# Fewer bit steps for the converted weights, and a new split of small steps over two engines, in a fused attention and two-layer expert kernel

## The chip, the core and the metric

The kernel runs on one core of a Trainium2 chip. The core has a matrix engine (TensorE, PE in the rows; its weight loads are PEld), a vector engine (VectorE, DVE), a scalar engine (ScalarE, ACT) and GpSimd (POOL). SyncE (SP) issues most of the DMA transfers. The metric is the device time of one execution in microseconds (us); lower is better. Each engine works through its own list of instructions in the order in which the program recorded them, so an instruction that has to wait holds up all that stand behind it on its engine.

## The reference, cut to what matters

```python
# q, k, v: (2, 8, 768, 64); x: 1536 tokens of 512 numbers
k_sum, v_sum = k in blocks of 32 .max, v in blocks of 32 .mean
scores = [scale * q k^T within a window of 16 | scale * q k_sum^T + log 32]
a = softmax(scores);  x = a @ [v | v_sum]
h = max(max(x @ w1, x @ w2), x @ w3);  x = h @ w_out        # these weights come as float64
score = x @ w_skip;  e = argmax(x @ w_gate)                 # 8 experts
out = x + gate * relu(x @ moe2_w1[e]) @ moe2_w2[e]   where score > 0, else x
```

The routing decides by sign and by largest value, so products are formed from split operands: each operand is a high part plus a low part, and a product is the three matmuls high·high, high·low and low·high.

## The kernel before, in words

**Stages.** The work comes in four groups of 384 tokens (u = 0 to 3). Per group there are four attention units (u, p) with two heads each. A unit is: scores on TensorE (`scores`), masking and row maximum on VectorE (`ttr`), exponentials on ScalarE (`ex`), sums inverted on VectorE (`rec`), normalisation (`norm`, L260), transposes on TensorE (`turn`, L265) with their evacuation (`turned`, L270), the product with the values (`pv`, L278; `fill_v`, L214, fills its summary rows), and the high and low part of the result (`put_h` L286, `put_l` L289). Then come 18 "chains" of 12 matmuls per group (L337: a weight tile (j, f), j = 0 to 2, f = 0 to 5, against the group's x), whose maximum over j gives h; `h_high` (L351) and `h_low` (L354) split h; and `x2_mm` (L364) multiplies by w_out. `route` sorts the tokens to experts and `scatter` (L536) writes their numbers to a table in device memory with indirect DMAs.

**Weight tiles.** 24 tiles of 128x512 float64 numbers (18 for w1 to w3, 6 for w_out) are turned into a float32 high part `wh` and low part `wl` on the chip, from the two 32-bit halves of each number. Per tile ScalarE makes the absolute value of the upper half (`w_c1`, L309) and the rounded top bits of the lower half (`w_r`, L305); a clamp follows on GpSimd (`w_cb`, L313); VectorE then shifts and masks (L317), puts the sign and exponent bit back (L318) and adds the lower bits as integers (L322); the high part is a copy (`w_c4`, L326) on ScalarE or GpSimd and the low part a subtraction on VectorE (`w_c5`, L330).

**What sets the order.** Every step is an entry of the list OPS with an engine. The table HOME names the engine for entries that can run on two (else ScalarE), and the table ORDER lists all entries in the order in which they are recorded. Both tables are constants. 20 entries are warm-up matmuls (`warm_up`, 63 matmuls of 512 columns in all, L159), which compute nothing that is used.

**Opening, middle, seam, last part.** Until 65 us the attention of groups 0 and 1 and the first weight tiles run side by side; the chains of group 0 begin there. After that the chains fill TensorE. At about 285 us the ordered part ends (the seam): the experts' chosen weight chunks (16, in `raw0` to `raw15`) have been split into `wh` and `wl` by `split` (L736, L738), in the buffers that the chains have freed, and the first `pair` starts. A pair puts 256 tokens through one expert: `first` (L1093) is 12 matmuls for each of eight column blocks, `second` (L1105) six each. It begins with the high and low part of the transposed tokens (`put_x`, xth on ScalarE, L712; xtl on VectorE, L713) and, at block 5, transposes the tokens of the next pair (`turn_x`, L705), which GpSimd has fetched by indirect DMA (`fetch`, L718). In GpSimd's list the three scatters of group 3 stand before that fetch. Its waits are for the transfer before.

Of the kernel before, what the change touches and what calls it, by code (L numbers as in the profile page):

```python
# [7 lines left out]
F32 = mybir.dt.float32  # L8
# [110 lines left out]
def build(tc, a, out):  # L119
# [138 lines left out]
    def norm(u, p, h):  # L258
        pr = ST["pr", u, p, h][0]
        nc.gpsimd.tensor_tensor(pr, pr, ST["se", u, p][:, h].unsqueeze(2).broadcast_to([P, TPG, KT]), ALU.mult)  # L260
# [50 lines left out]
    def w_cb(j, f):  # L311
        x = ST["cx", j, f]
        nc.gpsimd.tensor_scalar(x, x, HIGH, LOW, ALU.min, ALU.max)  # L313

# [1096 lines left out]
```

## Time and profile before

| what | us |
|---|---|
| three runs | 446.93, 448.0, 448.46 (median 448.0) |
| the profiled execution | 448.98 |
| its span, first to last instruction | 447.2 |
| PE busy in the span | 432.3 (97%) |
| DVE, ACT, POOL busy | 233.1, 184.3, 138.1 |
| share of PE in the chain that ended last | 83% |

The chain that ended last goes back from the last instruction to whatever released each step. Busy times of matmuls are modelled, so a PE that is called busy may still hold small waits. A "busy" duration of a DVE or ACT instruction overlaps the next one's by some 0.1 us.

### The profile page before, as it was taken

The numbers are of one execution on the slowest core, as the hardware profiler recorded it, in microseconds if no ns is written. First come the engines' busy times: TensorE is split into PE (matmuls) and PEld (weight loads), VectorE is DVE, ScalarE is ACT, GpSimd is POOL, SyncE is SP. The second block draws the span as 40 slices with busy tenths as digits, with TensorE's granted clock in tenths as the row PEclk, the third lists the DMA queues.
The fourth block names the chain that finished last, engine by engine and source line by source line (L and its number), as shares of the span: only waits on it lengthen the run. The fifth ranks groups of instructions, "written<-read, shape, count | busy, mean of one in ns | idle before, by whom it ended". The sixth has DMA issues, their size and how long they took to land.

```text
span 447.2 us, 9609 instructions
## 1 busy us (share of the span) xinstructions
PE 432.3 (97%) x3558; PEld 389.2 (87%) x3558; DVE 233.1 (52%) x738; ACT 184.3 (41%) x507; POOL 138.1 (31%) x191
## 2 busy tenths in 40 slices
PE   8999999999999999999999999799999999999995
PEld 3668889999789999998999999798989889798874
DVE  4899998989852531043214235868226651232321
ACT  3798984743685754107121037211114521212210
POOL 0666561434222522011601322131316034140400
PEclk9999999999999999999999999989999999999999
DMA  8987556456434512003042390242852193010111
GB/s 281 270 304 247 185 169 221 162 178 200 153 131 128 161 42 75 2 0 122 2 113 77 94 331 1 78 65 49 269 203 94 49 301 128 25 52 2 47 49 32
DMA packets 27584, 56.91 MB, mean 127 GB/s; under 512 B 6099, under 2 KB 8659, under 8 KB 27528
## 3 DMA queue, kind: packets, MB, share of 16 engines
q1 hardware_dynamic: 24968, 50.24, 35.3%
q0 software_dynamic: 2560, 5.96, 4.3%
q8 instruction: 30, 0.49, 0.5%
q14 instruction: 26, 0.21, 0.2%
HBM read 46.69 MB, written 10.47 MB: 128 GB/s over the span
## 4 chain that ended last, share of the span: by engine, by line
PE 83%; DVE 9%; ACT 3%; issue 2%; POOL 2%; DVEq 0%; ACTq 0%; POOLq 0%
PE pm L337 30%; PE ph L1093 13%; PE pm L1105 12%; PE pm L364 11%; PE ph L1186 2%; PE po L278 2%; DVE cx L318 2%; PE sc L226 2%; ACT pr L250 1%; PE pm L159 1%; PE pm L1158 1%; PE pt L265 1%; PE pm L1228 1%; DVE pr L243 1%; POOL pr L260 1%
## 5 line engine op out<-in xcount | busy, mean ns | idle before, releaser
L337 PE MATMUL pm<-xh,wh 128*128 128x384 f32 x288 | 65.2, 346 | 1.2 <-ACT t L344 0.7
L337 PE MATMUL pm<-xl,wh 128*128 128x384 f32 x288 | 62.2, 336 | 0.0
L337 PE MATMUL pm<-xh,wl 128*128 128x384 f32 x288 | 62.2, 335 | 0.0
L1096 ACT ACTIVATE hth<-ph 128x256 fp32r<-128x256 f32 x40 | 15.4, 384 | 91.4 <-PE ph L1093 84.8
L337 PEld LDWEIGHTS pm<-xh,wh 128*128 128x128 f32 x288 | 49.6, 188 | 3.5 <-ACT t L344 1.0
L337 PEld LDWEIGHTS pm<-xl,wh 128*128 128x128 f32 x288 | 51.1, 188 | 0.0
L337 PEld LDWEIGHTS pm<-xh,wl 128*128 128x128 f32 x288 | 51.1, 188 | 0.0
L1097 DVE SCALAR_TENSOR_TENSOR htl<-ph,hth 128x256 fp32r<-128x256 f32 x40 | 16.8, 422 | 56.3 <-ACT hth L1096 56.3
L346 DVE TENSOR_TENSOR t<-pm,t 128x384 f32<-128x384 f32 x48 | 26.1, 553 | 34.7 <-PE pm L337 34.5
L364 PE MATMUL pm<-wh,h 128*128 128x260 f32 (+1 forms) x288 | 43.5, 289 | 0.3 <-ACT x L386 0.3
L260 POOL TENSOR_TENSOR pr<-pr,se 128x360 f32<-128x360 f32 x32 | 27.0, 854 | 50.8 <-DVE se L256 33.1
L250 ACT ACTIVATE pr<-pr,mx 128x120 f32<-128x120 f32 x96 | 36.7, 386 | 12.5 <-DVE mx L243 12.3
L364 PEld LDWEIGHTS pm<-wh,h 128*128 128x128 f32 x288 | 38.2, 190 | 1.6 <-ACT x L386 0.5
L354 POOL TENSOR_TENSOR h<-t,h 128x384 fp32r<-128x384 f32 x24 | 25.3, 1069 | 32.5 <-ACT h L351 32.5
L1105 PE MATMUL pm<-wh,hth 128*128 128x512 f32 x80 | 31.9, 398 | 0.0
L1105 PE MATMUL pm<-wh,htl 128*128 128x512 f32 x80 | 31.6, 395 | 0.0
L1105 PE MATMUL pm<-wl,hth 128*128 128x512 f32 x80 | 31.3, 391 | 0.0
L718 POOL DMA_INDIRECT xn<-x2d,inx x14 | 14.9, 1063 | 48.6 <-DVE xm L1059 29.3
L243 DVE CUSTOM_DVE_ANT_0 pr<-sc,mask 128x120 f32<-128x120 f32 x96 | 21.1, 277 | 16.2 <-PE sc L226 14.1
L344 ACT COPY t<-pm 128x384 f32<-128x384 f32 x24 | 11.4, 478 | 39.9 <-PE pm L337 34.7
L1093 PE MATMUL ph<-xth,wl 128*128 128x256 f32 x160 | 26.2, 285 | 1.5 <-DVE wl L738 1.5
L1093 PE MATMUL ph<-xth,wh 128*128 128x256 f32 x160 | 26.6, 289 | 0.7 <-ACT xth L712 0.7
(337 smaller groups left out, 834.7 us busy)
## 6 DMA issues: line engine op xcount, KB each, us to landing
raw<-in_m SPq DMA_DIRECT2D x48, 256.0 KB, 5.0
raw<-in_wx SPq DMA_DIRECT2D x22, 512.0 KB, 4.3
vx<-in_vx SPq DMA_DIRECT2D x14, 288.0 KB, 3.5
qt<-in_qt SPq DMA_DIRECT2D x16, 192.0 KB, 4.1
raw<-in_vt SPq DMA_DIRECT2D x8, 384.0 KB, 5.9
x2d<-raw SPq DMA_DIRECT2D x12, 256.0 KB, 4.1
kx<-in_kx SPq DMA_DIRECT2D x8, 360.0 KB, 3.7
out<-raw SPq DMA_DIRECT2D x9, 256.0 KB, 3.2
```

Source lines behind the costliest of these rows:

```text
L243: nc.vector.tensor_tensor_reduce(pr[:, t, :], sc[:, t, :], mask[:, mv, :], -0.125, 3.0e38, ALU.add, ALU.min, mx[:, t:t + 1])
L250: nc.scalar.activation(pr[:, t, :], pr[:, t, :], AF.Exp, bias=mx[:, t:t + 1], scale=-1.0, accum_out=se[:, h, t:t + 1])
L260: nc.gpsimd.tensor_tensor(pr, pr, ST["se", u, p][:, h].unsqueeze(2).broadcast_to([P, TPG, KT]), ALU.mult)
L337: nc.tensor.matmul(ST["ch", u, f, j], l[j, f][:, c * P:(c + 1) * P], r[u][:, c, :], start=(cs[0] == 0 and n == 0), stop=(cs[-1] == KC1 - 1 ...
L346: nc.vector.tensor_tensor(ST["t1", u, f], ps, ST["t1", u, f], ALU.max)
L354: nc.gpsimd.tensor_tensor(HL[u, f], ST["t1", u, f], HH[u, f].bitcast(F32), ALU.subtract)
L364: nc.tensor.matmul(ps, l[u, f][:, t * P:(t + 1) * P], r[3, f][:, lo:hi], start=(part != 1 and n == 0), stop=(part != 0 and n == len(ops) - 1))
L718: nc.gpsimd.indirect_dma_start(out=xn[t], out_offset=None, in_=x2d, in_offset=bass.IndirectOffsetOnAxis(ap=inx[:, t, 0:1], axis=0), bounds ...
L1093: nc.tensor.matmul(ps, w[:, o:o + P], r[:, d, :], start=(n == 0), stop=(n == 3 * KC1 - 1))
L1096: nc.scalar.activation(hh, ps, AF.Relu)
L1097: nc.vector.scalar_tensor_tensor(hl, ps, 0.0, hh.bitcast(F32), ALU.max, ALU.subtract)
L1105: nc.tensor.matmul(py[i], l[:, o:o + P], r, start=(f == 0 and n == 0), stop=(f == 7 and n == 2))
```

## The change

The bit conversion of a tile needs one VectorE step less. The absolute value is now scaled by 2^-112 on ScalarE, so that the exponent field is already right, and the clamp has other limits. ScalarE's instruction for the lower half has a bias and rounds down. VectorE shifts and joins the lower bits in one step (L323 after) and puts the sign in with a second (L327 after). Four kinds of steps get an entry in HOME that they did not have (`nm` normalisation, `cb` clamp, `hl` low half of h; GpSimd where not named), and the entries of `c4`, `fv`, `ph`, `td` and all of ORDER are new.

```diff
 HOME = {
-    ("c4", "Pool"): [0, 1, 3, 6, 7, 8, 12, 19, 20, 22, 23],
-    ("fv", "Pool"): [(0, 0), (0, 1), (1, 2)],
-    ("ph", "DVE"): [(0, 0), (0, 2), (1, 1), (1, 2)],
-    ("td", "DVE"): [(0, 0, 1), (0, 2, 1), (1, 3, 1)],
+    ("c4", "Pool"): [0, 1, 3, 5, 6, 11, 23],
+    ("cb", "DVE"): [16, 17, 21],
+    ("fv", "Pool"): [(0, 0), (0, 1), (0, 3), (1, 3), (2, 0), (2, 1), (2, 3), (3, 1), (3, 3)],
+    ("hl", "DVE"): [(0, 0), (0, 1), (1, 0), (1, 1), (2, 0), (2, 2), (2, 3), (2, 4), (2, 5), (3, 0), (3, 1),
+        (3, 3), (3, 5)],
+    ("nm", "DVE"): [(0, 2, 1), (1, 0, 1), (1, 2, 1), (2, 2, 0), (2, 2, 1), (2, 3, 1), (3, 0, 0), (3, 0, 1),
+        (3, 1, 1), (3, 3, 1)],
+    ("ph", "DVE"): [(0, 1), (1, 2), (2, 0), (2, 1), (2, 2), (2, 3), (3, 0), (3, 1), (3, 2), (3, 3)],
+    ("td", "DVE"): [(0, 0, 0), (0, 0, 1), (0, 1, 1), (0, 2, 1), (0, 3, 1), (1, 1, 0), (2, 2, 1), (2, 3, 0),
+        (3, 0, 0), (3, 0, 1), (3, 1, 0), (3, 1, 1), (3, 3, 0)],
 }
 ORDER = [
-    5, 25, 27, 6, 49, 26, 7, 0, 51, 50, 8, 28, 34, 52, 35, 9, 37, 36, 10, 73, 29, 11, 38, 12, 76, 58, 39,
+    688, 3, 5, 27, 25, 4, 6, 49, 26, 7, 0, 28, 50, 34, 51, 37, 8, 73, 35, 38, 9, 29, 58, 52, 36, 10, 39, 75,
...
+    ENG = dict(Pool=nc.gpsimd, DVE=nc.vector)
...
     def norm(u, p, h):
-        nc.gpsimd.tensor_tensor(pr, pr, ST["se", u, p][:, h].unsqueeze(2).broadcast_to([P, TPG, KT]), ALU.mult)
+        ENG[HOME.get(("nm", (u, p, h)), "Pool")].tensor_tensor(pr, pr, ST["se", u, p][:, h].unsqueeze(2).broadcast_to([P, TPG, KT]), ALU.mult)
...
-    LOW = float(np.uint32(897 << 20).view(np.float32))
-    HIGH = float(np.uint32(1150 << 20).view(np.float32))
+    HIGH = float(np.uint32((255 << 20) - 1).view(np.float32))
...
     def w_r(j, f):
-        nc.scalar.mul(ST["cr", j, f], ST["raw", j, f][:, :, 0].bitcast(U32), 2.0 ** -29)
+        nc.scalar.activation(ST["cr", j, f].bitcast(U32), ST["raw", j, f][:, :, 0].bitcast(U32), AF.Copy, bias=-0.5 + 2.0 ** -21, scale=2.0 ** -29 * (1 - 2.0 ** -20))
...
     def w_c1(j, f):
-        nc.scalar.activation(ST["cx", j, f], ST["raw", j, f][:, :, 1].bitcast(F32), AF.Abs)
+        nc.scalar.activation(ST["cx", j, f], ST["raw", j, f][:, :, 1].bitcast(F32), AF.Abs, scale=2.0 ** -112)
...
     def w_cb(j, f):
-        nc.gpsimd.tensor_scalar(x, x, HIGH, LOW, ALU.min, ALU.max)
+        ENG[HOME.get(("cb", ws.index((j, f))), "Pool")].tensor_scalar(x, x, HIGH, 0.0, ALU.min, ALU.max)
...
     def w_c2(j, f):
-        nc.vector.tensor_scalar(xi, xi, 3, 0x3fffffff, ALU.logical_shift_left, ALU.bitwise_and)
-        nc.vector.scalar_tensor_tensor(xi, ST["raw", j, f][:, :, 1], -0x40000000, xi, ALU.bitwise_and, ALU.bitwise_or)
+        nc.vector.scalar_tensor_tensor(xi, xi, 3, ST["cr", j, f], ALU.logical_shift_left, ALU.bitwise_or)
...
     def w_c3(j, f):
-        nc.vector.tensor_tensor(xi, xi, ST["cr", j, f], ALU.add)
+        nc.vector.scalar_tensor_tensor(xi, ST["raw", j, f][:, :, 1], -0x80000000, xi, ALU.bitwise_and, ALU.bitwise_or)
...
     def h_low(u, f):
-        nc.gpsimd.tensor_tensor(HL[u, f], ST["t1", u, f], HH[u, f].bitcast(F32), ALU.subtract)
+        ENG[HOME.get(("hl", (u, f)), "Pool")].tensor_tensor(HL[u, f], ST["t1", u, f], HH[u, f].bitcast(F32), ALU.subtract)
```

Three places show what the two tables do to the lists of the engines. All line numbers of after are 5 to 7 higher than those of before.

VectorE in the opening, before, around its first finished tiles (cx is a tile in conversion, cr its lower bits, wl0_0 and wl1_1 finished low parts, ps a transposed score tile, xh and xl the attention result's parts):

```order
L322 ISA cx_443<-cx_443,cr_452 128x1024
L270 COPY ps1_517<-pt1_494 120x384
L330 TENSOR_TENSOR wl0_0_521<-cx_335,wh0_0_447 128x512
L286 CAST xh_371<-po_526 128x384
L317 TENSOR_SCALAR cx_510<-cx_510 128x512
L318 SCALAR_TENSOR_TENSOR cx_510<-raw_465,cx_510 128x512
L289 TENSOR_TENSOR xl_372<-po_526,xh_371 128x384
L330 TENSOR_TENSOR wl1_1_576<-cx_443,wh1_1_564 128x512
L322 ISA cx_510<-cx_510,cr_541 128x1024
L317 TENSOR_SCALAR cx_558<-cx_558 128x512
L318 SCALAR_TENSOR_TENSOR cx_558<-xh_505,cx_558 128x512
```

The same engine and stretch, after:

```order
L277 COPY ps1_462<-pt1_367 120x384
L323 SCALAR_TENSOR_TENSOR cx_406<-cx_406,cr_440 128x512
L327 SCALAR_TENSOR_TENSOR cx_406<-raw_353,cx_406 128x512
L262 TENSOR_SCALAR se_435<-se_435 128x6
L263 RECIPROCAL se_435<-se_435 128x6
L293 CAST xh_396<-po_474 128x384
L186 TENSOR_REDUCE vs_505<-raw_450 128x24
L277 COPY ps1_521<-pt1_508 120x384
L296 TENSOR_TENSOR xl_397<-po_474,xh_396 128x384
L323 SCALAR_TENSOR_TENSOR cx_490<-cx_490,cr_519 128x512
L327 SCALAR_TENSOR_TENSOR cx_490<-xh_408,cx_490 128x512
L335 TENSOR_TENSOR wl1_1_588<-cx_406,wh1_1_557 128x512
```

A tile's L317, L318, L322 have become L323, L327 there; an evacuation and the high part of another unit (L277, L293) stand among them.

VectorE at the seam, before, from the last small step of routing on (wl0_2 holds the low half of chunk 6, which the first 12 matmuls of the pair read, as they read wl0_0, wl2_0 and wl1_1):

```order
L531 COPY rw_3790<-pm_3867 1x16
L738 TENSOR_TENSOR wl1_4_3762<-raw13_3465,wh1_4_3761 128x512
L713 TENSOR_TENSOR xtl_3481<-ptx0_3474,xth_3480 128x4x128
L713 TENSOR_TENSOR xtl_3481<-ptx1_3475,xth_3480 128x4x128
L738 TENSOR_TENSOR wl2_3_3727<-raw11_3463,wh2_3_3726 128x512
L738 TENSOR_TENSOR wl0_2_3691<-raw6_3458,wh0_2_3690 128x512
L738 TENSOR_TENSOR wl0_1_3659<-raw3_3455,wh0_1_3658 128x512
L738 TENSOR_TENSOR wl0_3_3721<-raw9_3461,wh0_3_3720 128x512
L738 TENSOR_TENSOR wl1_0_3599<-raw1_3453,wh1_0_3598 128x512
```

The same place, after:

```order
L743 TENSOR_TENSOR wl1_2_3671<-raw7_3450,wh1_2_3670 128x512
L1064 COPY xm0_3968<-xn0_3467 128x512
L1064 COPY xm1_3969<-xn1_3468 128x512
L718 TENSOR_TENSOR xtl_3472<-ptx0_3465,xth_3471 128x4x128
L718 TENSOR_TENSOR xtl_3472<-ptx1_3466,xth_3471 128x4x128
L743 TENSOR_TENSOR wl2_4_3817<-raw14_3457,wh2_4_3816 128x512
L526 TENSOR_TENSOR rw_3770<-pm_3861,con_103 128x24
L527 TENSOR_TENSOR rw_3770<-rw_3770,roh_3775 128x24
L529 TENSOR_REDUCE rsl_3879<-rw_3770 128x3
L530 TENSOR_SCALAR rdo_3777<-rdo_3777 128x3
L532 TENSOR_TENSOR rsi_3882<-rsl_3879,rdo_3777 128x3
L536 COPY rw_3770<-pm_3858 1x16
```

Before, five splits stood behind xtl, wl0_2 among them; now one does, and wl0_2 stands further ahead, in a run before the routing of group 3. The routing's small steps (L526 to L536 after), which the scatters wait for, stood partly before xtl and now stand behind xtl and one split.

ScalarE at the seam, before, and after (x2 are output rows on their way to two DMAs each):

```order
L386 COPY x2_3821<-pm_3670 128x250
L388 COPY x2_3759<-pm_3768 128x262
L388 COPY x2_3821<-pm_3823 128x262
L712 CAST xth_3480<-ptx0_3474 128x4x128
L712 CAST xth_3480<-ptx1_3475 128x4x128
L388 COPY x2_3816<-pm_3845 128x262
```

After:

```order
L393 COPY x2_3738<-pm_3742 128x262
L741 CAST wh2_4_3816<-raw14_3457 128x512
L741 CAST wh0_5_3819<-raw15_3458 128x512
L393 COPY x2_3740<-pm_3796 128x262
L393 COPY x2_3763<-pm_3823 128x262
L717 CAST xth_3471<-ptx0_3465 128x4x128
L717 CAST xth_3471<-ptx1_3466 128x4x128
```

One of the copies of output rows stood behind xth, and now all stand ahead of it.

## Rows read from the trace of the kernel before

**Rows 1.** Stretches: length, then busy us of PE, PEld, DVE, ACT, POOL; PEclk, DMA, GB/s.

```profile
9.00:65.00 56.00, 52.59 (x641) 41.69 (x640) 52.92 (x175) 48.02 (x152) 32.95 (x45) 1.00 0.78 248
...
110.00:200.00 90.00, 89.56 (x874) 83.17 (x873) 38.18 (x184) 44.58 (x152) 21.61 (x29) 1.00 0.28 89
200.00:280.00 80.00, 78.82 (x575) 76.29 (x573) 25.93 (x99) 27.15 (x68) 22.69 (x25) 1.00 0.33 103
280.00:295.00 15.00, 12.52 (x94) 11.84 (x94) 10.50 (x29) 3.96 (x11) 2.73 (x3) 0.89 0.47 106
```

**Rows 2.** Timeline of PE in the opening: start, us, instruction, idle before and releaser.

```profile
61.30 0.54 PE L265 MATMUL pt<-ident,pr 128*120 128x128 f32 x3 [0.65 <-POOL pr L260]
```

**Rows 3.** DVE by line and form: count, busy us, mean ns, idle before.

```profile
L317 DVE TENSOR_SCALAR cx<-cx 128x512 int32<-128x512 int32 x24 | 11.1, 464 | 0.6 <-POOL cx L313 0.5
...
L318 DVE SCALAR_TENSOR_TENSOR cx<-raw,cx 128x512 int32<-128x512 int32 x22 | 18.2, 828 | 0.8
L322 DVE CUSTOM_DVE_ANT_0 cx<-cx,cr 128x1024 uint16<-128x1024 uint16 x24 | 17.6, 739 | 1.4 <-DVE cx L318 0.6 <-ACT cr L305 0.5
L330 DVE TENSOR_TENSOR wl<-cx,wh 128x512 fp32r<-128x512 f32 x24 | 17.5, 737 | 0.2 <-POOL wh L326 0.2
...
L270 DVE COPY ps<-pt 120x384 f32<-120x384 f32 x3 | 1.6, 543 | 0.2 <-PE pt L265 0.2
```

**Rows 4.** Timeline of DVE in the opening, one step twice.

```profile
33.33 0.98 DVE L318 SCALAR_TENSOR_TENSOR cx<-xh,cx 128x512 int32<-128x512 int32 x1
...
37.35 0.69 DVE L318 SCALAR_TENSOR_TENSOR cx<-raw,cx 128x512 int32<-128x512 int32 x1
```

**Rows 5.** POOL by line and form, the normalisation.

```profile
L260 POOL TENSOR_TENSOR pr<-pr,se 128x360 f32<-128x360 f32 x32 | 27.0, 854 | 50.8 <-DVE se L256 33.1 <-DVE lg L377 12.1 <-DVE xl L289 1.9
```

**Rows 6.** Timeline of POOL at the first step of rows 4.

```profile
33.73 1.63 POOL L313 TENSOR_SCALAR cx<-cx 128x512 f32<-128x512 f32 x2
```

**Rows 7.** Timeline of PE at the seam and in the first pair.

```profile
287.00 0.74 PE L1093 MATMUL ph<-xth,wh 128*128 128x256 f32 x4 [0.72 <-ACT xth L712]
...
289.60 0.58 PE L1093 MATMUL ph<-xth,wl 128*128 128x256 f32 x1 [1.50 <-DVE wl L738]
...
294.63 0.40 PE L1105 MATMUL pm<-wh,hth 128*128 128x512 f32 x1
...
307.24 1.03 PE L705 MATMUL ptx<-ident,xn 128*128 128x128 f32 x8
```

**Rows 8.** Timeline of DVE at the seam.

```profile
286.03 0.18 DVE L524 TENSOR_REDUCE rsl<-rw 128x3 f32<-128x24 f32 x1
...
287.08 1.27 DVE L713 TENSOR_TENSOR xtl<-ptx,xth 128x512 fp32r<-128x512 f32 x2
288.28 3.08 DVE L738 TENSOR_TENSOR wl<-raw,wh 128x512 fp32r<-128x512 f32 x5
```

**Rows 9.** Stretches behind the seam: columns as in rows 1, GB/s last.

```profile
290.00:292.00 2.00, 2.00 (x11) 2.00 (x11) 1.78 (x4) 0.39 (x1) 0.48 (x1) 0.50 1.49 158
...
306.00:306.50 0.50, 0.50 (x4) 0.41 (x3) 0.43 (x3) 0.38 (x1) 0.00 (x0) 1.00 0.04 16
```

**Rows 10.** Timeline of ACT at the seam.

```profile
285.88 1.07 ACT L712 CAST xth<-ptx 128x512 fp32r<-128x512 f32 x2 [2.74 <-PE ptx L705]
```

**Rows 11.** Chain of waits in the first pair: start, us, what.

```profile
296.18 1.42 PE ph L1093 x12
```

**Rows 12.** Timeline of POOL: scatters of groups 2 and 3.

```profile
242.69 0.97 POOL L536 DMA_INDIRECT table<-rtab,rsi  x1 [3.03 <-DMA table<-rtab,rsi]
...
286.76 1.30 POOL L536 DMA_INDIRECT table<-rtab,rsi  x1 [1.28 <-DVE rw L531]
291.52 1.00 POOL L536 DMA_INDIRECT table<-rtab,rsi  x1 [3.46 <-DMA table<-rtab,rsi]
298.17 0.98 POOL L536 DMA_INDIRECT table<-rtab,rsi  x1 [5.64 <-DVE hq L624]
```

**Rows 13.** Timeline of SP's queue: transfers of output rows.

```profile
287.26 1.37 SPq L381 DMA_DIRECT2D out<-x  x3
```

More of the change, by code (lines that the diff above doesn't have):

```diff
@@ L858, in build @@
         op(("cq",) + w, "ACT", 0.67, t + 0.15, w_r, j, f, after=[("c1",) + w], take=[("cr", ("cr",) + w)], uses=[("rw",) + w])
-        op(("c2",) + w, "DVE", 1.05, t + 0.1, w_c2, j, f, after=[("cb",) + w], uses=[("rw",) + w])
-        op(("c3",) + w, "DVE", 0.62, t + 0.2, w_c3, j, f, after=[("c2",) + w, ("cq",) + w], uses=[("cr",) + w])
+        op(("c2",) + w, "DVE", 0.62, t + 0.17, w_c2, j, f, after=[("cb",) + w, ("cq",) + w], uses=[("cr",) + w])
+        op(("c3",) + w, "DVE", 0.62, t + 0.2, w_c3, j, f, after=[("c2",) + w], uses=[("rw",) + w])
         put(("c4",) + w, n, dict(ACT=0.62, Pool=0.66), t + 0.3, w_c4, j, f, after=[("c3",) + w])
```

90 rows, old and new, of the table ORDER are left out of this document.

## The prediction

> **What bounds the kernel now.** I read the stretches first, then the timelines of the engines where TensorE stands still. TensorE is called busy for all but 1.62 us of the 170 us between 110 and 280 [rows 1], and its matmuls are not touched by the change. So time can be won only where it waits, and that is in two places. In the opening (9 to 65 us) it is idle for 56.00 - 52.59 = 3.41 us [rows 1], in pieces such as the 0.65 us before a transpose that waits for GpSimd's normalisation [rows 2]. VectorE is busy there for 52.92 of 56 us (94%), ScalarE for 48.02 (86%), GpSimd for 32.95 [rows 1]: the opening goes at VectorE's pace, although the names behind TensorE's waits differ. From 280 to 295 TensorE is idle for 2.48 us and its mean granted clock is 0.89 [rows 1]: that is the seam. The warm-up matmuls stay 63 and are no reserve unless real work displaces them, which a fixed order doesn't allow.
>
> **The change part by part: the opening.** I compare the work in VectorE's list up to the last low part of group 1's attention, with the ten weight tiles that both orders finish by then.
> - The bit steps: L317, L318 and L322 take 464 + 828 + 739 = 2031 ns a tile [rows 3]. After, two steps join two tensors, as L318 does; the trace has no shift joined to an or, so each is bounded by L318's 690 ns with GpSimd quiet and its 980 ns beside it [rows 4]. I take the mean, 828. That is 1656 a tile, 375 less, and for ten tiles -3.75 us (between -6.5 and -0.7).
> - Moved evacuations: transposed scores on VectorE go from three to six, high parts of the result from four to two. At 543 ns for the former [rows 3], and as much for the latter, of the same size, that is +1.63 - 1.09 = +0.54 us.
> - Three normalisations come to VectorE. No row shows one there: from above GpSimd's own 854 ns bounds it [rows 5], from below L317's rate, 464 x 360/512 = 326 ns. I take L330's rate, since it also reads two tensors in SBUF: 737 x 360/512 = 518 ns [rows 3]. Three are +1.55 us (1.0 to 2.6).
>
> The sum for VectorE is -3.75 + 0.54 + 1.55 = -1.66 us, and I take the opening as 1.7 us shorter. GpSimd has three normalisations less (-2.6 us), and one fill of summary rows more in exchange for one copy, so it doesn't become the bound. ScalarE's list loses three evacuations, gains two high parts and one weight copy, and loses a fill; at 86% it hides that. The two ScalarE instructions per tile keep their size, and I cost the new scale and bias at nothing; were they slower, ScalarE's idle 8 us would hide 0.3 us on each of the 20 or so.
>
> The Trainium skill (GPSIMD Engine Reference, Key points) says that GpSimd shares its SBUF interfaces with VectorE and contends with VectorE instructions in a two-port mode or with two SBUF inputs. The trace agrees: L318 took 0.98 us beside two clamps that took 1.63 us, and 0.69 us later on [rows 4, 6]. By that rule all the new bit steps stay exposed; the first rival is what that could come to.
>
> **The middle.** From 65 us on the chains feed TensorE without a gap, and the engines behind it have slack: from 110 to 200 VectorE is busy for 42%, ScalarE for 50% [rows 1]. Clamps, low halves of h and late evacuations that change engine there I cost at nothing; what hides them is that slack. If the cover fails, it is the third rival. The 1.62 us of idle time may come or go, ±1.5 us.
>
> **The seam.** Before, the pair's first 12 matmuls begin at 287.00 and stop until 289.60 for a low part from VectorE [rows 7]; it is wl0_2, second in the run of five splits behind xtl [rows 8]. TensorE then goes at half its clock (0.50 from 290 to 292) [rows 9], and the first `second` begins at 294.63 [rows 7]. After, all four low parts that this group reads stand ahead of the routing of group 3; what remains is xtl. ScalarE ends xth at 285.88 + 1.07 = 286.95 [rows 10], a half of xtl takes about 0.65 [rows 8], so xtl is there at 287.6, just before TensorE has done the eight matmuls ahead of it (287.00 + 8/12 x 1.42 = 287.95). At full clock 12 matmuls take 1.42 us [rows 11], so three groups end at 287.00 + 4.26 = 291.26: 3.4 us earlier than 294.63.
>
> What is late next is GpSimd. Its scatters wait for the routing's small steps, which now follow xtl (287.6) and a split (3.08/5 = 0.6) and are six of some 0.18 us, like the one at 286.03 [rows 8], 1.1 us: ready at about 289.4 against 286.76 [rows 12], 2.6 us later, while TensorE comes 3.4 us earlier. Behind three scatters stands the fetch of the tokens that TensorE transposes at 307.24 [rows 7]. The transfers are quiet from 306.0 on [rows 9], so before there are 1.2 us of slack. The scatters start 4.76 and 6.65 us apart, each waiting for the transfer before; in a quiet time they are 4.0 apart [rows 12]. I read the longer gaps, 4.76 and 6.65, as the output rows' transfers, which are queued from 287.26 on, six in two lines of three like this one [rows 13]. ScalarE's copies for these now all stand ahead of xth, so the last goes out earlier by xth's 1.07 us and more. With 4.76 and 4.0 the third scatter starts at 298.2, as before, and TensorE transposes at 306.0 instead of 307.24: 1.3 us won (1.2 us of slack used). With two quiet gaps it is 2.0, with the old gaps the transpose comes at 308.6, 1.4 us late. The seam's range is thus +1.4 to -3.4 (all of it kept); I take -1.3.
>
> **Sum.** -1.7 - 1.3 = -3.0 us. The profiled execution took 448.98 us with a span of 447.2, so 445.98; that execution was 1.0 us above the median of the runs, 448.0, and against the median it is 445.0 us. This is 0.7% less; what a measurement here can tell from no change is about 0.3%, 1.3 us.
>
> **The rivals.**
> 1. *Contention takes the opening's gain.* If the two steps of every tile meet GpSimd (980 ns each), ten tiles cost 3.0 us more: the opening is 3.04 - 1.66 = 1.4 us longer and the total 448.0 - 1.3 + 1.4 = 448.1. For it speaks the pair of rows on L318 [rows 4]; against it, that GpSimd has less to do.
> 2. *The seam is handed back.* With the old gaps between the scatters the seam costs 1.4 us, and a TensorE that stands still for over 4 us there may fall to half clock again, as it did from 290 on; a group of 12 then costs up to 1.42 us more [rows 11], and I take 1.0: 448.0 - 1.7 + 2.4 = 448.7.
> 3. *Slower: VectorE holds up the chains of groups 2 and 3.* All eight high parts of these groups and seven evacuations of scores now stand in VectorE's list, where none stood, among the maxima of the chains. An evacuation waits for a matmul that may stand far down TensorE's list, and the maximum behind it waits too; with three buffers for chains TensorE stops when two more are done. At 0.7 us a stop, the size of the opening's transposes' wait [rows 2], ten of 15 stops cost 7.0 us: 448.0 - 3.0 + 7.0 = 452.0. It decides from five stops on, which eat the gain. Against it: VectorE was busy for 32% between 200 and 280 [rows 1].
> 4. *More is won.* TensorE's waits in the opening vanish (3.4 us) and the seam is kept whole (3.4): 441.2. That the bit steps are not fewer is excluded by the order of after, which has two rows for each tile.
>
> **How the numbers follow.** I give the forecast 0.43 (its own range 443.2 to 446.6), rival 1 0.17, rival 2 0.12, rival 3 0.15, rival 4 0.13. Faster by over 0.3% (under 446.7): 0.41 + 0.06 + 0.03 + 0.13 = 0.63 of these. Within 0.3%: 0.02 + 0.08 + 0.06 + 0.03 = 0.19. Slower: 0.03 + 0.03 + 0.12 = 0.18. The range that leaves out some of rival 3 and the best end of rival 4 is 441.2 to 449.8.
>
> **What the profile after would show.** The two new steps at 0.69 to 0.98 us, 24 of each; TensorE's idle time from 9 to 65 us near 2 us; the pair's first 12 matmuls without a wait for a low part and at granted clock 1.00; a wait before the second `turn_x`, released by the fetch. The prediction is wrong if the opening keeps its 3.4 us of idle time, if TensorE waits between 110 and 280 for more than 3 us, or if the fetch comes later than before.

## The result: 8.0 us faster, 2.7 times what was forecast

The changed kernel took 440.19 us (439.94 to 440.3, four runs), the kernel before 448.23 in all its runs then: ratio 0.982, 95% interval 0.9801 to 0.9839. Forecast were 445.0 us, and a range from 441.2. The direction was right, the size and the range were not. The profiled execution took 440.16 us with a span of 438.2, so 9.0 us less span than before. Two later runs of the same program, beside before on other chips, were 6.9 and 7.4 us faster.

Stretches of after, columns as in rows 1:

```profile
9.00:65.00 56.00, 55.52 (x657) 45.55 (x658) 51.49 (x165) 48.02 (x151) 29.11 (x38) 1.00 0.82 254
65.00:110.00 45.00, 45.00 (x299) 44.27 (x296) 36.56 (x72) 28.13 (x61) 12.74 (x16) 1.00 0.63 194
110.00:200.00 90.00, 89.43 (x863) 84.31 (x864) 46.23 (x196) 35.98 (x135) 17.31 (x21) 1.00 0.32 94
200.00:280.00 80.00, 79.71 (x608) 78.30 (x604) 37.80 (x121) 25.49 (x60) 14.44 (x17) 1.00 0.29 92
280.00:295.00 15.00, 14.83 (x103) 13.57 (x103) 11.87 (x70) 2.31 (x6) 5.52 (x9) 1.00 0.23 80
```

Before, from 65 to 110 us, which [rows 1] leaves out:

```profile
65.00:110.00 45.00, 45.00 (x267) 44.52 (x267) 40.48 (x67) 25.31 (x49) 16.51 (x21) 1.00 0.56 184
```

Against [rows 1]: from 9 to 65 us TensorE's idle time fell from 3.41 to 0.48 us, and its weight loads (the second of the busy times, PEld) rose from 41.69 to 45.55 us: 3.86 us more work in the same 56 us. From 200 to 280 us PEld rose by 2.01, from 110 to 200 by 1.14. Together that is 7.0 us, less 0.25 lost from 65 to 110: 6.8 us. The last of the 72 chains shows the same without weight loads. VectorE starts its maximum 6.8 us earlier, before:

```profile
271.30 0.56 DVE L346 TENSOR_TENSOR t<-pm,t 128x384 f32<-128x384 f32 x1 [1.52 <-PE pm L337]
```

and after:

```profile
264.50 0.56 DVE L351 TENSOR_TENSOR t<-pm,t 128x384 f32<-128x384 f32 x1 [0.26 <-PE pm L342]
```

The first pair starts at 279.24 instead of 287.00, 7.8 us earlier; of the 1.0 us that came in between, 0.43 is the shorter wait for xth (0.29, before 0.72).

TensorE at the seam, after (start, us, instruction, idle before and releaser); before is [rows 7]:

```profile
279.24 0.74 PE L1098 MATMUL ph<-xth,wh 128*128 128x256 f32 x4 [0.29 <-ACT xth L717]
279.82 0.63 PE L1098 MATMUL ph<-xth,wl 128*128 128x256 f32 x4
280.62 0.74 PE L1098 MATMUL ph<-xtl,wh 128*128 128x256 f32 x4 [0.17 <-DVE xtl L718]
...
284.02 0.39 PE L1110 MATMUL pm<-wh,hth 128*128 128x512 f32 x1
...
298.38 1.29 PE L710 MATMUL ptx<-ident,xn 128*128 128x128 f32 x8 [1.63 <-DMA xn<-x2d,inx]
```

The wait for wl0_2 is gone, and a short one for xtl (0.17) stands there. The first `second` comes 4.78 us after the first matmul of the pair (before 7.63). Then TensorE waits 1.63 us for the fetch. From the pair's first matmul to the second turn it took 20.24 us, now 19.14: 1.1 us won, 1.3 forecast. Before's 20.24 holds its stretch at half clock [rows 9]; what that means for the 1.1 stands under The seam.

GpSimd there, after; before is [rows 12]:

```profile
282.24 1.03 POOL L541 DMA_INDIRECT table<-rtab,rsi  x1 [4.10 <-DVE rw L536]
286.87 0.99 POOL L541 DMA_INDIRECT table<-rtab,rsi  x1 [3.59 <-DMA table<-rtab,rsi]
290.93 0.97 POOL L541 DMA_INDIRECT table<-rtab,rsi  x1 [3.07 <-DVE p_fr L647]
291.89 0.21 POOL L1057 COPY ic<-im 128x4 int32<-128x4 int32 x1
292.02 1.17 POOL L1059 COPY xr<-xm 128x512 f32<-128x512 f32 x2
293.12 0.18 POOL L1113 COPY inx<-in 128x4 int32<-128x4 int32 x1
293.58 1.06 POOL L723 DMA_INDIRECT xn<-x2d,inx  x1 [0.27 <-POOL inx L1113]
```

The scatters start 4.63 and 4.06 us apart, where 4.76 and 4.0 were forecast; the first comes 3.0 us after the pair's first matmul (2.4 forecast), behind the small steps. Then follow copies of the rows in hand (1.17 us) and the fetch.

VectorE by line and form, after; before is [rows 3, 5]:

```profile
L323 DVE SCALAR_TENSOR_TENSOR cx<-cx,cr 128x512 int32<-128x512 int32 x24 | 18.7, 784 | 1.1 <-POOL cx L319 0.7 <-ACT cr L311 0.2
...
L327 DVE SCALAR_TENSOR_TENSOR cx<-raw,cx 128x512 int32<-128x512 int32 x22 | 15.3, 702 | 0.2
...
L277 DVE COPY ps<-pt 120x384 f32<-120x384 f32 x13 | 7.0, 546 | 6.9 <-PE pt L272 6.9
L267 DVE TENSOR_TENSOR pr<-pr,se 128x360 f32<-128x360 f32 x10 | 7.0, 699 | 0.1
```

The two steps are 784 and 702 ns (828 was taken for each), the normalisation 699 (518 was taken, GpSimd needs 846 to 854).

### The profile page after: what moved, and what is told of

Same layout as the page of the kernel before. It is cut to its first block, busy times and chain, and to the rows that moved or that the text cites. A ratio compares the mean times of both kernels' runs of the same rounds, so it can differ in the third digit from the quotient of the medians.

```text
span 438.2 us, 9563 instructions
## 1 busy us (share of the span) xinstructions
PE 427.4 (98%) x3558; PEld 387.3 (88%) x3558; DVE 241.3 (55%) x756; ACT 174.8 (40%) x489; POOL 117.8 (27%) x167
## 4 chain that ended last, share of the span: by engine, by line
PE 87%; DVE 5%; DMA 3%; issue 1%; POOL 1%; ACT 1%; SPq 0%; POOLq 0%; DVEq 0%; ACTq 0%
PE pm L342 33%; PE pm L369 12%; PE ph L1098 11%; PE pm L1110 11%; PE po L285 3%; PE ph L1191 3%; PE pt L272 2%; PE sc L233 2%; PE pm L166 2%; PE pm L1163 1%; PE sc L238 1%; DMA raw<-in_kt 1%; DMA h<-in_kt 1%; PE pm L1233 1%; PE ptx L710 1%
## 5 line engine op out<-in xcount | busy, mean ns | idle before, releaser
L267 POOL TENSOR_TENSOR pr<-pr,se 128x360 f32<-128x360 f32 x22 | 18.4, 846 | 43.8 <-DVE se L263 43.1
L541 POOL DMA_INDIRECT table<-rtab,rsi x12 | 12.0, 998 | 58.3 <-DMA table<-rtab,rsi 25.5
L1098 PE MATMUL ph<-xtl,wh 128*128 128x256 f32 x160 | 25.3, 279 | 0.2 <-DVE xtl L718 0.2
L1098 PEld LDWEIGHTS ph<-xth,wh 128*128 128x128 f32 x160 | 23.0, 188 | 2.7 <-issue 0.4
L1098 PE MATMUL ph<-xth,wl 128*128 128x256 f32 x160 | 25.2, 279 | 0.0
```

What stands on the lines that cost most here:

```text
L267: ENG[HOME.get(("nm", (u, p, h)), "Pool")].tensor_tensor(pr, pr, ST["se", u, p][:, h].unsqueeze(2).broadcast_to([P, TPG, KT]), ALU.mult)
L1098: nc.tensor.matmul(ps, w[:, o:o + P], r[:, d, :], start=(n == 0), stop=(n == 3 * KC1 - 1))
```

## Experiments

Three theories. **1:** the opening goes at VectorE's pace; the work taken off VectorE is the gain. **2:** the order of the lists is the gain. **3:** the choice of engines is. A fourth, 2b, came out of the first four runs: each of the three pays only with the others. The table has all runs in the order of the text. Idle is TensorE's from 9 to 65 us; PEld is the busy time of its weight loads in four stretches, the measure of how much work got done in each. All come from the stretches of each run's profiled execution; the time is the median, the ratio is to the kernel before on the same chip.

| kernel | us | ratio (95%) | idle | PEld 9–65 | 65–110 | 110–200 | 200–280 |
|---|---|---|---|---|---|---|---|
| before | 448.2 | 1 | 3.41 | 41.69 | 44.52 | 83.17 | 76.29 |
| after | 440.2 | 0.982 (0.980–0.984) | 0.48 | 45.55 | 44.27 | 84.31 | 78.30 |
| a_three: three bit steps | 447.9 | 1.001 (0.999–1.004) | 3.33 | 42.03 | 40.20 | 84.43 | 78.23 |
| b_two: before, two bit steps | 448.0 | 0.999 (0.997–1.001) | 3.12 | 42.50 | 43.80 | 82.39 | 76.76 |
| a_home0: default engines | 446.6 | 0.997 (0.995–0.998) | 4.08 | 41.64 | 43.15 | 83.71 | 77.81 |
| a_order0: old order | 453.0 | 1.011 (1.008–1.015) | 5.81 | 40.30 | 42.96 | 81.24 | 77.05 |
| a_home1: engines of before | 443.8 | 0.989 (0.986–0.992) | 1.09 | 44.37 | 43.58 | 83.94 | 78.10 |
| a_late0: late engines of before | 443.7 | 0.990 (0.987–0.993) | 1.29 | 44.72 | 43.92 | 83.41 | 78.23 |
| a_first: new order to 122 us | 446.5 | 0.995 (0.993–0.997) | 0.60 | 45.55 | 44.34 | 82.46 | 77.69 |
| a_second: new order from 122 us | 453.0 | 1.009 (1.006–1.013) | 5.91 | 39.93 | 43.03 | 79.81 | 78.19 |
| b_noadd: before, one step left out | 444.4 | 0.992 (0.988–0.995) | 1.60 | 44.63 | 44.06 | 83.08 | 77.06 |
| b_two_cq: b_two, lower bits earlier | 448.1 | 0.999 (0.997–1.001) | 2.31 | 42.60 | 44.52 | 82.59 | 76.27 |
| b_seam: before, new seam order | 446.6 | 0.998 (0.996–1.000) | 3.42 | 41.66 | 44.52 | 83.18 | 76.70 |
| a_again: after once more | 441.8 | 0.985 (0.982–0.988) | 1.20 | 45.08 | 44.23 | 84.30 | 78.06 |
| a_fetch | 439.5 | 0.981 (0.978–0.983) | 0.49 | 45.11 | 44.27 | 84.52 | 78.22 |
| a_fetch2: a_fetch once more | 440.6 | 0.983 (0.980–0.986) | 1.27 | 45.07 | 44.17 | 84.36 | 78.05 |
| a_scat | 438.7 | 0.979 (0.977–0.982) | 1.37 | 44.71 | 44.02 | 84.73 | 78.17 |
| a_again2: after, beside a_scat | 440.6 | 0.984 (0.981–0.987) | 1.01 | 45.22 | 44.27 | 84.47 | 78.11 |

### One part undone, or one part alone

**a_three**, after with three steps (the sign joins last, because in this order the lower bits' buffer is given free early; the instructions on ScalarE and the clamp are those of before too):

```diff
...
-        nc.vector.scalar_tensor_tensor(xi, xi, 3, ST["cr", j, f], ALU.logical_shift_left, ALU.bitwise_or)
+        nc.vector.tensor_scalar(xi, xi, 3, 0x3fffffff, ALU.logical_shift_left, ALU.bitwise_and)
+        nc.vector.tensor_tensor(xi, xi, ST["cr", j, f], ALU.add)
-        nc.vector.scalar_tensor_tensor(xi, ST["raw", j, f][:, :, 1], -0x80000000, xi, ALU.bitwise_and, ALU.bitwise_or)
+        nc.vector.scalar_tensor_tensor(xi, ST["raw", j, f][:, :, 1], -0x40000000, xi, ALU.bitwise_and, ALU.bitwise_or)
```

Expected: 

> The changed kernel with the three bit steps of before (shift and mask, add of the lower bits, join of the sign), order and engines of after. Theory 1 (the opening goes at VectorE's pace, so what counts is VectorE's work): 2031 - 1486 = 545 ns a tile come back, about ten tiles stand in the opening, so about 5 us, 445 us, and TensorE's idle time from 9 to 65 us is back above 2 us. Theory 2 (the gain lies in the order of the lists): within 1.5 us of 440.2. Theory 3 (the choice of engines): likewise within 1.5 us.

All of the gain is lost. The stretches of a_three:

```profile
9.00:65.00 56.00, 52.67 (x617) 42.03 (x619) 52.81 (x172) 45.41 (x146) 25.98 (x36) 1.00 0.75 227
65.00:110.00 45.00, 42.29 (x285) 40.20 (x284) 41.92 (x72) 27.03 (x50) 12.84 (x16) 1.00 0.57 189
```

VectorE is at 52.81 of 56 us and then at 41.92 of 45 (93 to 94%), and TensorE idles 3.33 and 2.71 us: with the longer steps the new order runs behind VectorE until 110 us. Theories 2 and 3 as put are out.

**b_two**, before with two steps, where the sign goes into the lower bits first and ten tiles have the first step moved behind ScalarE's lower bits:

```diff
...
-        nc.vector.tensor_scalar(xi, xi, 3, 0x3fffffff, ALU.logical_shift_left, ALU.bitwise_and)
-        nc.vector.scalar_tensor_tensor(xi, ST["raw", j, f][:, :, 1], -0x40000000, xi, ALU.bitwise_and, ALU.bitwise_or)
+        cr = ST["cr", j, f]; nc.vector.scalar_tensor_tensor(cr, ST["raw", j, f][:, :, 1], -0x80000000, cr, ALU.bitwise_and, ALU.bitwise_or)
-        nc.vector.tensor_tensor(xi, xi, ST["cr", j, f], ALU.add)
+        nc.vector.scalar_tensor_tensor(xi, xi, 3, ST["cr", j, f], ALU.logical_shift_left, ALU.bitwise_or)
```

Expected: 

> The kernel before with two bit steps and nothing else (ten tiles have the first step moved behind ScalarE's lower bits, which it now reads; it joins the sign to the lower bits first). Theory 1: the opening gains what VectorE loses, up to 5 us, so 443 to 445 us. Theory 2: the order still fixes the waits, 446.5 to 448.5. Theory 3: the same as theory 2.

No gain, as theory 2 had it, though VectorE has 5.0 us less to do in the opening (47.95 against 52.92). What VectorE waits for there, in all rows 8.2 us; b_two (total, times, longest):

```profile
DVE pr L243 <- PE sc L231: 2.4, 4, 1.6
DVE cr L316 <- ACT cr L304: 2.3, 3, 1.6
DVE se L255 <- ACT pr L250: 2.0, 3, 1.0
```

Before, all rows together are 2.3 us, and none is for the lower bits:

```profile
DVE se L255 <- ACT pr L250: 0.6, 1, 0.6
...
DVE pr L243 <- PE sc L231: 0.4, 2, 0.2
```

The freed time has become waits: for scores that TensorE makes when its own list comes to them, for ScalarE's exponentials, and for its lower bits, which three-step tiles need only in the third step.

**a_home0** was meant to have the engines of before. Its table HOME was written in a form in which no entry is found: all switchable steps ran on their default engine.

```diff
-    ("c4", "Pool"): [0, 1, 3, 5, 6, 11, 23],
...
+    ('c4', 0): 'Pool',
+    ('c4', 1): 'Pool',
...
 HOME = {(n, i): e for (n, e), v in HOME.items() for i in v}
```

Expected: 

> The changed kernel with the engines of before for every step that can run on two (normalisation, clamp and low half of h all on GpSimd, high parts, evacuations, copies and fills as before), order and bit steps of after. Theory 3 (the choice of engines, above all for the attention of group 3, shortens the chain that TensorE waits for): TensorE waits again for GpSimd's normalisation and ScalarE's evacuations, 443 us or more, with new idle time between 200 and 240 us. Theory 1: VectorE has even less to do in the opening, 439 to 441. Theory 2: 440 to 442.

ScalarE has the evacuations, copies and fills alone, is busy for 53.14 of 56 us in the opening, and TensorE idles 4.08 there. It says what no shifting costs, not what the new choice is worth.

**a_order0**, ORDER of before with the engines and two steps (as in b_two) of after. Expected: 

> The changed kernel's engines and bit steps in the order of before. Theory 2 (order): the waits at their old places come back, 446 us or more. Theory 1: 443 to 445, with the seam's 1.3 us and some of the middle lost. Theory 3: 441 to 443.

5 us slower than before, although VectorE is busy for 47.97 us only. What TensorE waits for in the opening (total, times, longest):

```profile
PE po L285 <- ACT ps L277: 2.2, 2, 1.3
...
PE pm L342 <- DVE t L351: 0.8, 1, 0.8
```

These are a score tile's evacuation by ScalarE and a chain's maximum on VectorE, which, as I read it, now stand behind other work in lists that were ordered for other engines and durations. With a_three and a_home0 this makes theory 2b.

### Which engines, which stretch of the order

**a_home1** and **a_late0** differ from after in HOME alone: all of it as before, or only groups 2 and 3 and the low halves of h. The diff is that of a_home1, cut:

```diff
-    ("cb", "DVE"): [16, 17, 21],
-    ("hl", "DVE"): [(0, 0), ...
-    ("nm", "DVE"): [(0, 2, 1), ...
+    ("c4", "Pool"): [0, 1, 3, 6, 7, 8, 12, 19, 20, 22, 23],
+    ("fv", "Pool"): [(0, 0), (0, 1), (1, 2)],
+    ("ph", "DVE"): [(0, 0), (0, 2), (1, 1), (1, 2)],
+    ("td", "DVE"): [(0, 0, 1), (0, 2, 1), (1, 3, 1)],
```

Expected: 

> The changed kernel with exactly the engines of before for all switchable steps (the run a_home0 had all of them on their default engine: copies, fills, evacuations and high parts on ScalarE, the rest on GpSimd). Order and bit steps of after. Theory 2b (an order pays only with the engines and steps that it was written for): 444 to 447, with waits in the opening for GpSimd's normalisation. Theory 2 (order alone): 440 to 442.

Expected: 

> The changed kernel, but groups 2 and 3 of the attention and all low halves of h on the engines of before; the opening's engines stay those of after. Both runs with the new order had no wait of TensorE at the two places between 200 and 240 us where before has 0.72 and 0.46 us. If the order took these away, they stay away and the time is 440 to 441.5; if VectorE's part in these groups did it, they come back: 442 to 443. If the opening's engines make the difference of a_home0, this run is near 440.

443.8 and 443.7: the engines are worth some 2 to 3.6 us (after took 440.2, 441.8 and 440.6 on three chips), and nearly all of that is the late part, since a_home1 is no slower than a_late0. The forecast had costed the late part at nothing. The two waits that before has at 203 and 233 us (TensorE, before):

```profile
PE pm L337 <- ACT t L344: 0.7, 1, 0.7
PE pm L337 <- ACT raw L370: 0.5, 1, 0.5
```

did not come back; so the order took those away, and the expectation was wrong on where the engines count: TensorE idles 1.32 us from 110 to 200, in after 0.57. The table divides the two. From 110 to 200 PEld is 84.3 to 84.7 with after's engines and order throughout, whatever the bit steps, and 83.4 to 83.9 in the same order with other engines. From 200 to 280 it is 77.8 to 78.3 with the new order there, whatever the engines, and 76.3 to 77.7 with the old. Which of the late steps does it was not tried.

**a_first** and **a_second** have after's engines and steps, the new order up to entry 560 and the old one from there, or the reverse.

Expected: 

> The changed kernel (its engines and bit steps throughout), with its order up to the last weight tile (entry 560 of 979, about 122 us) and the order of before from there on. If what the order gives adds up by stages, the waits between 200 and 240 us (2 us of gaps) and part of the seam (1.2 us) come back: 443 to 444.5. If the late order is worth nothing by itself: 440 to 441.5.

Expected: 

> The reverse: the order of before up to the last weight tile, the new order from there on, engines and bit steps of after. a_order0 was 452.95 with the old order throughout; if the late part is worth 3 to 4 us by itself, this is 449 to 450, with the opening's waits of a_order0 (5.8 us of idle time from 9 to 65 us); if the old opening is what costs, it can't be below 448.

The opening of a_first is that of after (PEld 45.55), its time is the sum expected only in some executions. The four shortest of ten, 443.4 (the profiled one) to 445.2 us, had a mean granted clock of 0.998 to 1.00, the six others, 446.3 to 447.9, one of 0.991 to 0.996; where they lost it no trace shows. The late order behind the old opening is worth nothing: a_second is as slow as a_order0. It has PEld 78.19 from 200 to 280 as after has, but loses as much where the orders meet (79.81 from 110 to 200, a_order0 81.24). So what a part of an order is worth depends on the part before it.

### Does VectorE bound the old opening?

**b_noadd**, before without L322; nothing takes its place.

```diff
-        nc.vector.tensor_tensor(xi, xi, ST["cr", j, f], ALU.add)
```

Expected: 

> The kernel before without the third bit step: the add of the lower bits (L322) is left out, so the weights lose bits below 2 to the -21 of their value; nothing is put in its place and nothing new is waited for. VectorE has 739 ns less for each of 24 tiles, about 7.4 us in the opening. Theory 1 (the opening goes at VectorE's pace): 3 to 6 us faster than before, 442 to 445. Theory 2b (the lists' order fixes when things can start; free time on VectorE turns into waits there): within 1.3 us of before, and TensorE's idle time from 9 to 65 us stays near 3 us.

3.7 us faster. Stretch of b_noadd:

```profile
9.00:65.00 56.00, 54.40 (x652) 44.63 (x657) 49.56 (x172) 50.64 (x157) 32.17 (x45) 1.00 0.79 252
```

So theory 1 holds where nothing new is waited for: 7.4 us less on VectorE for ten tiles give 2.9 us more weight loads in the opening. The step left out is also the one that reads the lower bits, so a wait of 0.5 us for these goes with it [rows 3]. VectorE's pace is a bound of the old opening, at about half its price.

**b_two_cq**, b_two with ScalarE's lower bits moved ahead in ORDER for the ten tiles. Expected: 

> b_two with one difference: in the ten tiles whose first bit step stood ahead of ScalarE's lower bits, the lower bits are moved ahead in ScalarE's list and the first bit step keeps its old place in VectorE's. If VectorE's waits for the lower bits ate the gain of two steps, most of it comes back: b_noadd took 739 ns a tile away and won 3.7 us, this takes 545 ns, so about 2.7 us, 445 to 446. If the lower bits moved ahead hold up ScalarE's list by as much (each takes 0.7 us), or if two steps are worth nothing in the old order for another reason, within 1.3 us of before.

Within noise of before again (before took 449.0 on that chip), though idle time fell to 2.31. VectorE waits there for

```profile
DVE cr L316 <- ACT cr L304: 4.1, 4, 1.3
```

4.1 us: moving the lower bits to just ahead of the step was not enough, ScalarE's list is late by more. In after, VectorE's waits in the whole opening are 3.8 us in all rows, among them

```profile
DVE pr L250 <- PE sc L238: 0.9, 2, 0.7
...
DVE cx L323 <- ACT cr L311: 0.2, 1, 0.2
```

so 0.2 us for the lower bits, and for the scores less than half as long as in b_two. That these waits eat the gain of two steps in the old order is thus supported; a run without them in the old order was not made.

### The seam

**b_seam**, the low halves, routing, output rows and scatters of group 3 in the relative order of after, in before. Expected: 

> The kernel before with one part of the new order: the low halves of the chunks, the routing of group 3, its output rows and scatters stand in the relative order of after, in the places that they held. The forecast's seam term: from the first turn of tokens to the second 22.0 us become 20.7 to 20.9, the wait for wl0_2 goes and a wait for the fetch comes; 446.7 us. The rival (it is handed back): 448 or more.

The second turn comes at 305.37 instead of 307.24, with a wait of 1.96 us for the fetch. The profiled execution, 448.96 us, lost it again; its stretch from 296 us:

```profile
296.00:312.00 16.00, 14.04 (x77) 12.04 (x76) 12.04 (x58) 2.50 (x6) 5.86 (x10) 0.89 0.20 39
```

The mean clock is 0.89. Six of the ten executions took 445.9 to 446.6; the median, 446.57, is 1.2 us below before on that chip, as forecast, but the ratio's interval reaches 1.000. The same in **a_again** (after unaltered), where the second turn

```profile
299.44 1.29 PE L710 MATMUL ptx<-ident,xn 128*128 128x128 f32 x8 [2.02 <-DMA xn<-x2d,inx]
```

is followed by half clock (0.51, about 1.2 of 2.4 GHz):

```profile
301.00:303.00 2.00, 2.00 (x11) 2.00 (x10) 0.00 (x0) 0.05 (x1) 0.00 (x0) 0.51 0.07 1
```

Expected: 

> The changed kernel unaltered, for a comparison with a_fetch2 on one chip: 440.2 by all theories.

It took 441.8. In the first profile of after the wait was 1.63 us and the clock stayed at 1.00. So a wait for the fetch can cost more than its own length; the forecast had this as part of its second rival.

The length of a wait alone doesn't decide it. b_two_cq has the lists of before at the seam, and the same wait for wl0_2, but keeps its clock:

```profile
289.36 0.39 PE L1091 MATMUL ph<-xth,wl 128*128 128x256 f32 x1 [1.51 <-DVE wl L736]
...
305.50 1.03 PE L703 MATMUL ptx<-ident,xn 128*128 128x128 f32 x8
```

```profile
290.00:292.00 2.00, 2.00 (x19) 2.00 (x19) 1.45 (x3) 0.71 (x2) 1.00 (x1) 1.00 1.43 114
```

The clock is 1.00 where before has 0.50 [rows 9]. From the pair's first matmul (286.76) to the second turn it takes 18.74 us, in before 20.24: the half clock costs 1.5 us. a_order0 and a_first, with the order of before at the seam, waited 1.50 and 1.51 us and kept the clock too (18.74 and 18.69 us). The executions of before itself differ so: on one chip five with a mean granted clock of 0.998 to 1.00 took 447.05 to 447.77 us, twelve with 0.995 or 0.996 took 448.31 to 450.64. After needs 19.14, 19.43 and 18.23 us for this way in three profiles (after, a_again, a_again2). So at full clock the new order of the seam is no shorter on this way. What it wins over the profile of before is the half clock, and time ahead of the pair: that of b_seam starts at 285.82, that of before at 287.00.

**a_fetch** moves GpSimd's fetch ahead of the copies in the first pair, and one split behind the routing's small steps; **a_scat** leaves the split where after has it and moves the fetch ahead of the three scatters too. The diff is that of a_scat, cut:

```diff
     def pair(p, t, spl=0, gen=None, sc=()):
-        begin(2)
+        begin(2) if not gen else None
...
-            nc.gpsimd.tensor_copy(inx, M2["in2"])
-            fetch()
+            nc.gpsimd.tensor_copy(inx, M2["in2"]); fetch(); begin(2)
+            [scatter(NG - 1, i) for i in sc]
```

Expected: 

> The changed kernel with two moves at the seam: in the first pair GpSimd fetches the next pair's tokens before it copies the rows of the present one (two copies, 1.3 us), and the last split of a chunk stands behind the routing's small steps instead of ahead (0.6 us). If the fetch's chain sets the wait of 1.63 us before the second turn, the wait goes and the time is 438.6 to 439.0; if the copies are needed in time for the first pair's end, or the fetch waits for the scatters' transfers anyway, 440.2.

It took 439.5, and the wait was 0.50 us. In three profiles of after unaltered it was 1.63, 2.02 and 0.72 us, so that alone shows no gain. Beside a_again on one chip, as a_fetch2:

Expected: 

> a_fetch unaltered, beside a_again on one chip. In the single executions the second turn came 19.67 us after the first instead of 20.90 us, so it should be faster by 0.7 to 1.2 us; if the 0.5 us of wait that is left or the opening's variation takes that, no difference.

440.6 against 441.8, with ranges that overlap (440.05 to 442.7, 440.56 to 443.79), and a wait of 1.07 us: a gain is not shown.

Expected: 

> The changed kernel with the fetch of the second pair's tokens ahead of the three scatters of group 3 (and of the copies of the present rows) in GpSimd's list; it then no longer waits for the routing nor for the scatters' transfers. If that chain sets the wait before the second turn (1.63 us in the trace of after, with half the clock behind it in some executions), the wait goes altogether: second turn 19.2 us after the first instead of 20.9 and a spread like that of the first four runs of after: 438.3 to 439.0. If the scatters, 3 us later, hold up the third pair's tokens, the third turn waits instead and the time is 440 or more.

438.67 us (438.38 to 439.36), beside after on the same chip (a_again2) 440.63 (439.74 to 441.39): 2.0 us faster, and the fastest kernel here. GpSimd and the second turn in a_scat:

```profile
287.20 1.04 POOL L723 DMA_INDIRECT xn<-x2d,inx  x1 [7.23 <-DVE p_pk L620]
288.55 1.00 POOL L723 DMA_INDIRECT xn<-x2d,inx  x1 [0.31 <-DVE hq L629]
289.56 0.20 POOL L1057 COPY ic<-im 128x4 int32<-128x4 int32 x1
289.69 1.16 POOL L1059 COPY xr<-xm 128x512 f32<-128x512 f32 x2
291.02 1.04 POOL L541 DMA_INDIRECT table<-rtab,rsi  x1 [0.17 <-DVE hqt L636]
295.48 0.99 POOL L541 DMA_INDIRECT table<-rtab,rsi  x1 [3.43 <-DMA table<-rtab,rsi]
299.30 0.97 POOL L541 DMA_INDIRECT table<-rtab,rsi  x1 [2.82 <-DMA table<-rtab,rsi]
```

```profile
297.25 0.40 PE L1110 MATMUL pm<-wh,htl 128*128 128x512 f32 x1
297.49 1.04 PE L710 MATMUL ptx<-ident,xn 128*128 128x128 f32 x8
```

The fetch goes out at 287.20 and the turn has no wait. The scatters are up to 9 us later than in after (the third at 299.30), and the third turn doesn't wait for them. From the pair's first matmul to the second turn it takes 17.36 us, in a_again2 18.23, with a wait of 0.72: of the 2.0 us between the medians the two traces show 0.9 there, and not where the rest is.

## Why the forecast was wrong, point by point

**The step that failed is the first one:** "time can be won only where it waits". I took TensorE's idle time (3.41 us in the opening, 1.62 from 110 to 280) as all there was to win, and so put the best case at 441.2. But in the profile, which models the ends of matmuls, a matmul's row goes on after the next one has started. Four matmuls of a chain in after stand for 0.85 us and start every 0.69 us:

```profile
37.03 0.85 PE L342 MATMUL pm<-xh,wl 128*128 128x384 f32 x4
37.73 0.85 PE L342 MATMUL pm<-xh,wh 128*128 128x384 f32 x4
38.42 0.85 PE L342 MATMUL pm<-xl,wh 128*128 128x384 f32 x4
```

One row is some 0.33 us long, and the next starts after 0.17. A gap shorter than what is left of the last row doesn't show as idle time. PEld shows it: it was busy for 41.69 of 56 us in [rows 1], and for 44.52 of 45 from 65 to 110, so there was room for far more than 3.41. The Trainium skill (Perfetto Trace Analysis, Identifying the Most-Contended Engine) says that matmul busy time is not a good measure of TensorE's headroom, and that the busy share of weight loads is one. The trace agrees: PEld rose by 3.86 us where idle time fell by 2.93, and by 2.01 us from 200 to 280 where it fell by 0.89.

**The opening, -1.7 us, was mis-sized:** PEld says 3.9. The bit steps cost 784 + 702 = 1486 ns instead of 1656, which is 1.7 us more for ten tiles; the three normalisations cost 0.5 us more than taken. But the sum's form was wrong too. b_two takes 5.0 us off VectorE and wins nothing; b_noadd takes some 7 and wins 3.7. What VectorE saves counts only as far as its list finds its inputs ready. The waits say that in after they nearly are (0.2 us for the lower bits, 0.9 for the scores), in the old order with two steps less so (2.3 and 2.4 in b_two).

**The middle, taken as 0, won 2.9** (1.14 + 2.01 - 0.25 in PEld). The two waits for ScalarE, 1.2 us, went in every run with the new order throughout; the first, 0.72 us, stayed in b_two. The new order gave the gain from 200 to 280, the late engines that from 110 to 200; a_late0 as a whole is 2 to 3.6 us slower than after. The forecast let slack hide these engines. It had no term at all for the seven late normalisations that went to VectorE.

**The seam, -1.3 us, was right in its steps:** the wait for the low part gone, a wait for the fetch in its place, the scatters 4.63 and 4.06 us apart. That its size came out, 1.1 us, is in part luck. The forecast took the half clock behind 290 us as fixed; the same lists at full clock need 18.7 us where after needs 18.2 to 19.4. And it had no term for the earlier start of the pair, which the seam's order alone brings (1.2 us in b_seam).

**The sum** of the profiled executions is 3.9 + 2.9 + 1.0 (from 280 to the first pair) + 1.1 = 8.9 of the 9.0 us of span. None of the forecast's three signs of being wrong came; all of them were about winning too little.

**The rivals.** Contention (1): no; L318's successors are shorter in the mean. Handed back (2): not in the first profile, but its half clock appeared in a_again, behind a wait of 2.02 us. VectorE holds up groups 2 and 3 (3): no; VectorE's busy time from 200 to 280 us rose from 25.93 to 37.80 us and TensorE's idle time fell to 0.29. More is won (4), given 0.13, was the case, with 440.2 beyond its own bound of 441.2. None of the rivals had it that a part of the change alone is no faster than before (b_two), or that two parts are slower (a_order0): the forecast treated the three tables as separate terms that add.

## What to carry to other kernels

Judge TensorE's room by the busy time of its weight loads, not by its idle time: short gaps hide in the rows of the matmuls ahead of them. With fixed lists, look at the steps' durations, the engines and the order as one thing: a shorter step put into an order made for the longer one may win nothing, since the next wait stands right behind it. Where one engine's list carries a fetch behind work that it doesn't need, look there first: that was worth 2.0 us of median here for a few moved lines. And don't count a half clock behind a short wait as a fixed price: the same wait had it in one execution and not in another.

## What the runs showed that I had not expected

A stop of TensorE of 1.50 us was followed by half clock (0.50) in before, one of 1.51 by none in b_two_cq; in the program of after one of 2.02 was (0.51), one of 1.63 was not. The same program's opening varies: in three executions of after the idle time from 9 to 65 us was 0.48, 1.20 and 1.01 us, mostly in the wait for the first maxima. And leaving out a step of 739 ns a tile in the old order won more (3.7 us) than shortening three steps to two by 545 ns (nothing).
